# Moving the softmax weights and one combine of a two-part decode attention ahead of the last V group

## Chip, cores, metric

One core of a Trainium2 chip. The metric is device time in microseconds (us) of one execution. A time comes with a span, which is the time from the first to the last instruction of the core's profile. In all executions of this study the time is the span plus 1.7 to 2.0 us.

## The reference

Two decode attentions, A and B, each for one token. Each has 32 query heads, 16 key/value heads, head size 128 and model size 576. B attends to all 8192 cached positions, A to the last 2048. The outputs are concatenated.

```python
q = (x @ wq).reshape(B, Sq, Hq, Dh).transpose(0, 2, 1, 3)
k = repeat(k_cache[:, :, Sk - W:, :], rep)      # A: W = 2048; B: everything
v = repeat(v_cache[:, :, Sk - W:, :], rep)
p = softmax(einsum("bhqd,bhkd->bhqk", q, k) * Dh ** -0.5)
o = einsum("bhqk,bhkd->bhqd", p, v)
out = o.transpose(0, 2, 1, 3).reshape(B, Sq, Hq * Dh) @ wo
```

The inputs that must be read are 102.8 MB, nearly all of it K and V.

## The kernel before

The kernel streams K and V in slots of 2 MB, four slots to a group, five groups (A is group 0, B is groups 1 to 4). All loads are issued from one queue (SP). PE, the matmul engine, runs the groups in a loop. The loop has an inner part for K (transposes and scores, under a condition) and an outer part for V:

```python
inner = sorted(p for p in body if body[p].loop[2] is not None)
with eng.Fori(0, self.outer) as v:
    with eng.Fori(*self.rounds_of(v)) as g:
        while inner:
            ...                                  # K parts, each under its condition
    some(sorted(p for p in body if body[p].loop[2] is None))   # the V group
```

After each V group, DVE (the vector engine) extracts the useful blocks from PSUM (the memory that PE writes to) into `acc`:

```python
def v_keep(g):
    def go(dve): ...                             # diag <- opsum * mask, 0.69 us
    add("dve", go, reads=[B_O, "rows"], writes=[("diag", g % 2)])
    sums(acc[:, g, :], diag[:, g % 2, :, :], ...)  # acc <- diag, 0.69 us
```

Softmax statistics of each chunk are known long before. `weights(P)` turns them into factors. It is a chain of tiny steps that go back and forth between PE, DVE and ACT (the scalar engine):

```python
def weights(P):                                  # cut to the steps
    add("pe", ... misc[0:1, 0:128] <- transpose of the chunk maxima)
    add("dve", ... maximum over partitions); add("dve", ... scale, 4 small ops)
    add("pe", ... misc[:, 128:129] <- back to partitions); add("dve", ... copy)
    add("act", ... exp); add("dve", ... times the sums)
    add("pe", ... misc[:, 130:131] <- total over partitions)
    add("dve", ... reciprocal); add("dve", ... factors)
```

`combine(P)` scales and adds `acc` of the chunks on DVE, and gathers the heads with four fp32 matmuls. `wo_part` is the output projection, 128 short matmuls for each of A and B. Everything after the loop stands in this order:

```python
for P, lo, n, view, res, after in wo_loads:      # 3 loads of A's wo, 6 of B's
    load_wo(P, lo, n, view, res, after)          # into K and V slots that are free
weights(0)
weights(1)
for P in range(2):
    combine(P)
    for Q, lo, n, view, res, after in wo_loads:
        if Q == P:
            wo_part(P, lo, n, view, res)
    finish_out(P)
```

## Time and profile before

| | before |
|---|---|
| time, median of the first 3 runs (lowest to highest) | 251.45 us (251.21 to 251.67) |
| time of the run that was profiled | 252.97 us |
| span of the profiled run | 251.2 us |
| loads | 102.77 MB |
| last load lands | 245.30 us |

First the profile's slices, of the kernel before: busy tenths of PE, then the granted PE clock (tenths of full speed), the DMA engines' busy share (tenths) and the rate, in 40 slices of 6.3 us.

```profile
PE   0183799984999359995999349996353433543766
PEclk9999689999999759999999857999659555555556
DMA  7999999999999999999999999999999999999980
GB/s 274 396 432 422 432 425 428 417 436 428 428 427 423 428 420 436 421 431 428 431 423 431 431 431 423 431 431 428 425 428 436 423 433 425 433 418 425 423 332 3
```

The loads run at one rate from the second slice to the last but two.

Next the chain that ended last, of the kernel before: start us, us, what.

```profile
225.92 0.69 DVE acc L366
...
232.58 1.02 PE misc L597 x4
...
234.31 1.93 PE misc L620 x8
...
236.60 4.05 PE ktps L636 x120
...
242.40 1.93 PE misc L620 x8
...
244.68 4.06 PE ktps L636 x96
...
248.76 0.31 DVE outsb L642
```

The last V group has been extracted at 226.6. The weights of A and B take until 234.0, A's combine (L620) until 236.5, A's projection (L636) until 240.65; then the same two for B. The output store follows the last line. All of this is compute. No load stands in this chain.

Last, the loads of B's wo, of the kernel before: the first line has the shortest, median and longest time of issue (ns), then the first and last issue (us); the second the time from issue to landing.

```profile
L373 SPq DMA_DIRECT2D vslots<-in_B_wo_dram x5: 327/433/4230, 210.8 to 216.4; - x5
...
DMA to landing us min/median/max: 28.8/30.1/32.0
```

The last of these five, issued at 216.4, lands 28.9 us later, at 245.3: it queues behind other loads, of which the one before it lands at 244.95. The projection of B, which needs it, begins its first matmul at 244.68 and needs the last piece at about 248.6.

### The profile page before, as it was taken

The page shows a single profiled execution, that of the slowest core. Times are in us where ns is not written, and L with a number is a line of the kernel's source. Part 1 is how long each engine was busy: PE and PEld are TensorE (multiplying, and loading weights), DVE is VectorE, ACT ScalarE, POOL GpSimd, SP SyncE. Part 2 cuts the span into 40 slices and gives each one's busy share as a digit, 9 for nine tenths or more (in the row PEclk, how much of TensorE's full clock was granted, in tenths as well). Part 3 has the DMA queues.
Part 4 walks back from the last instruction along what each step waited for, and adds up shares of the span by engine and source line. Part 5 has one row for each costly group of instructions (what it writes and reads, how often), then busy time and mean ns, then how long its engine had stood idle before and what let it go on. Part 6 is the DMA issues. An engine that isn't in the chain of part 4 may idle for free. (4 is left out here: it accounts for less than half of the span.)

```text
span 251.2 us, 7501 instructions
## 1 busy us (share of the span) xinstructions
PE 167.9 (67%) x3406; PEld 130.6 (52%) x3406; DVE 80.6 (32%) x152; ACT 86.7 (35%) x92; POOL 12.9 (5%) x49
## 2 busy tenths in 40 slices
PE   0183799984999359995999349996353433543766
PEld 0031287764776358865776349783242322432755
DVE  0000244664653035554654024653031020014120
ACT  2000067839683027877676007874000000000000
POOL 7501000000000000000000000000000000000000
PEclk9999689999999759999999857999659555555556
DMA  7999999999999999999999999999999999999980
GB/s 274 396 432 422 432 425 428 417 436 428 428 427 423 428 420 436 421 431 428 431 423 431 431 431 423 431 431 428 425 428 436 423 433 425 433 418 425 423 332 3
DMA packets 8235, 102.92 MB, mean 410 GB/s; under 512 B 1184, under 2 KB 1312, under 8 KB 2080
## 3 DMA queue, kind: packets, MB, share of 16 engines
q1 hardware_dynamic: 7936, 102.77, 96.7%
q8 instruction: 8, 0.13, 0.2%
q10 hardware_dynamic: 288, 0.00, 0.1%
q14 instruction: 3, 0.02, 0.0%
HBM read 102.76 MB, written 0.00 MB: 409 GB/s over the span
## 5 line engine op out<-in xcount | busy, mean ns | idle before, releaser
L465 ACT ACTIVATE kt<-ktps 128x1024 bf16<-128x1024 bf16 x80 | 77.5, 1021 | 53.2 <-PE ktps L459 53.2
L459 PEld LDWEIGHTS ktps<-ident,kslots 128*128 128x128 bf16 x1280 | 76.3, 101 | 28.8 <-issue 28.8
L459 PE MATMUL ktps<-ident,kslots 128*128 128x128 bf16 x1280 | 82.4, 226 | 12.8 <-PEq L213 12.8
L468 DVE COPY kt<-ktps 128x1024 bf16<-128x1024 bf16 x80 | 55.2, 691 | 52.1 <-PE ktps L459 52.0
L550 PE MATMUL opsum<-vslots,ptm 128*32 128x128 bf16 x1280 | 29.9, 268 | 39.7 <-PEq L213 39.3
L550 PEld LDWEIGHTS opsum<-vslots,ptm 128*32 128x32 bf16 x1280 | 26.3, 121 | 44.2 <-issue 44.1
L479 PE MATMUL sacc<-kt,qst 128*32 128x512 bf16 x320 | 25.9, 392 | 2.0 <-PEq L213 1.8
L559 DVE TENSOR_TENSOR diag<-opsum,rows 128x512 f32<-128x512 f32 x5 | 3.5, 691 | 68.0 <-PE opsum L550 68.0
L589 ACT ACTIVATE stat<-stat 128x1 f32<-128x1 f32 (+1 forms) x2 | 0.6, 295 | 56.7 <-DVE stat L587 56.7
L418 PE MATMUL opsum<-vslots,xpad 128*32 128x512 bf16 x64 | 8.3, 497 | 16.1 <-DVE xpad L403 12.2
L418 PEld LDWEIGHTS opsum<-vslots,xpad 128*32 128x32 bf16 x64 | 2.2, 116 | 18.9 <-issue 13.1
L450 POOL COPY qst<-qtm 128x64 bf16<-128x64 bf16 x20 | 4.5, 236 | 122.8 <-PE sacc L479 113.3
L479 PEld LDWEIGHTS sacc<-kt,qst 128*32 128x32 bf16 x320 | 5.4, 94 | 8.7 <-issue 4.8
L424 ACT ACTIVATE qrow<-opsum 128x512 bf16<-128x512 f32 x2 | 1.2, 597 | 24.8 <-PE misc L418 24.8
L516 ACT ACTIVATE psb<-sacc,stat 128x2048 bf16<-128x2048 f32 x3 | 5.9, 1967 | 8.5 <-DVE stat L510 8.5
L418 PE MATMUL misc<-vslots,xpad 128*32 128x512 bf16 x64 | 8.4, 500 | 0.0
L426 DVE CAST qrow<-misc 128x512 bf16<-128x512 f32 x2 | 1.4, 690 | 16.2 <-PE misc L418 16.2
L636 PE MATMUL ktps<-kslots,opj 128*32 128x144 bf16 x184 | 5.9, 326 | 0.7 <-DVE opj L624 0.7
L636 PEld LDWEIGHTS ktps<-kslots,opj 128*32 128x32 bf16 x184 | 5.4, 146 | 1.0 <-issue 1.0
L620 PE MATMUL misc<-acc,pick 128*128 128x32 f32 x16 | 3.8, 404 | 2.5 <-DVE acc L614 1.8
L620 PEld LDWEIGHTS misc<-acc,pick 128*128 128x128 f32 x16 | 3.6, 328 | 2.9 <-DVE acc L614 2.1
L508 DVE TENSOR_REDUCE stat<-sacc 128x1 f32<-128x1024 f32 x3 | 3.7, 1225 | 1.8 <-PE sacc L479 1.8
(66 smaller groups left out, 57.7 us busy)
## 6 DMA issues: line engine op xcount, KB each, us to landing
kslots<-in_B_k_cache_dram SPq DMA_DIRECT2D x16, 2048.0 KB, 21.4
vslots<-in_B_v_cache_dram SPq DMA_DIRECT2D x16, 2048.0 KB, 18.1
kslots<-in_A_k_cache_dram SPq DMA_DIRECT2D x4, 2048.0 KB, 30.0
vslots<-in_A_v_cache_dram SPq DMA_DIRECT2D x4, 2048.0 KB, 24.7
vslots<-in_A_wq_dram SPq DMA_DIRECT2D x2, 2048.0 KB, 10.0
vslots<-in_B_wq_dram SPq DMA_DIRECT2D x2, 2048.0 KB, 20.2
kslots<-in_A_wo_dram SPq DMA_DIRECT2D x2, 2016.0 KB, 23.8
kslots<-in_B_wo_dram SPq DMA_DIRECT2D x1, 2016.0 KB, 31.2
```

The costliest lines, as they stand in the source:

```text
L418: ins = pe.matmul(qps[c][32 * j:32 * j + 32, :], lhsT=xpad[:, P, x, :], rhs=src[:, o:o + 512], start=(u == 0), stop=(u == WQ_UNITS - 1))
L450: add("pool", lambda pool: pool.tensor_copy(qst[:, s * 64:(s + 1) * 64], qtm[:, o:o + 64]), reads=[("qtm", KIND[g])], writes=[("qst", s)], ...
L459: ins = pe.matmul(ktps_bf[q][:, t * 128:(t + 1) * 128], lhsT=kslots[:, s, o:o + 128], rhs=ident[:, :], start=True, stop=True, is_transpose ...
L465: add("act", lambda act, q=q, dst=dst: act.activation(dst, ktps_bf[q], ACT.Copy), reads=[("bank", q)], writes=[("kt", u % NKT, q)], tag="e ...
L468: add("dve", lambda dve, q=q, dst=dst: dve.tensor_copy(dst, ktps_bf[q]), reads=[("bank", q)], writes=[("kt", u % NKT, q)], tag="e%d%d" % ( ...
L479: ins = pe.matmul(sacc[32 * j:32 * j + 32, 512 * half:512 * half + 512], lhsT=qst[:, s * 64 + e * 32:s * 64 + e * 32 + 32], rhs=rhs, start ...
L508: add("dve", lambda dve: dve.tensor_reduce(st(P, C_M + k), sacc[:, :], AX.X, ALU.max), reads=B_S, writes=[("st", P, C_M + k)], tag="max")
L516: return act.activation(psb[:, :].rearrange("p (x g) -> p x g", g=2), src, ACT.Exp, bias=st(P, C_NB + k), scale=SCALE, accum_out=st(P, C_L ...
L550: ins = pe.matmul(opsum[32 * j:32 * j + 32, s * DH:(s + 1) * DH], lhsT=ptm[:, o:o + 32], rhs=vslots[:, s, b * 128:(b + 1) * 128], start=(u ...
L559: return dve.tensor_tensor(diag[:, g % 2, :, :], opsum[:, :].rearrange("p (s d) -> p d s", s=NS), m, ALU.mult)
L620: ins = pe.matmul(misc[:, 0:32], lhsT=pick[:, r, :], rhs=acc[:, d, 32 * r:32 * r + 32], start=(r == 0), stop=(r == 3))
L636: ins = pe.matmul(ktps[P][32 * j:32 * j + 32, 0:OUTW], lhsT=opj[:, P, jj:jj + 32], rhs=view[:, o:o + OUTW], start=(jj == 0), stop=(jj == H ...
```

## The change

The weights of A and B and A's combine need nothing from the last V group. The change places them ahead of it. PE is then waiting for V loads anyway (in the profile of the kernel before it stands idle for 2.7 to 3.3 us ahead of each of the last four V slots). Since PE runs a loop, they become a conditional part of the loop's outer body, taken only in the last round. B's combine now comes before A's projection. No load and no arithmetic is added or removed. The core of the diff:

```diff
-            inner = sorted(p for p in body if body[p].loop[2] is not None)
+            def parts(of, i):
+                ...                          # runs of places with the same condition
+                        with eng.If(cond(i)):
+                            some(todo[:n])
             with eng.Fori(0, self.outer) as v:
                 with eng.Fori(*self.rounds_of(v)) as g:
-                    while inner:
-                        ...
-                some(sorted(p for p in body if body[p].loop[2] is None))
+                    parts("inner", g)
+                parts("outer", v)
 ...
+    LAST = lambda v: v == 4
     def weights(P):
+        at = [(6, 18 + P + k / 8, LAST, "outer") for k in range(3)]
 ...                                          # loop=at[0], at[1], at[2] on its three PE steps
-        add("pe", mm, reads=["pick", ("acc", d)], writes=[B_M])
+        add("pe", mm, reads=["pick", ("acc", d)], writes=[B_M], loop=(6, 19.5, LAST, "outer") if P == 0 else None)
 ...
+        if g == 6:
+            weights(0)
+            weights(1)
+            combine(0)
         if g in V_OF:
             for s in range(NS):
                 v_slot(V_OF[g], s, 20 + s, g)
 ...
-    weights(0)
-    weights(1)
+    combine(1)
     for P in range(2):
-        combine(P)
         for Q, lo, n, view, res, after in wo_loads:
```

The rest of the diff lets the bookkeeping of the loop's semaphore waits cope with the new places.

More of the change, by code (lines that the diff above doesn't have):

```diff
@@ L134, in waits_of_loop @@
     def waits_of_loop(self, ops):
-        points, state, tried = {}, [], {}
+        points, state, body = {}, [], {op.loop[1] for op in ops}
         for op in ops:
@@ L145, in waits_of_loop, with fits @@
             dma = key[0] == "dma"
-            runs = {p: sum(1 for q, _, _ in state if q == p) for p in places}
-            taker = max(places, key=lambda p: (runs[p], p))
-            def fits(first, n):
+            runs = {p: sum(1 for q, _, _ in state if q == p) for p in body}
+            def fits(first, n, places, taker):
                 took = 0
@@ L175, in waits_of_loop @@
                 continue
-            fit = [(first, n) for n in (1, 2, 16) for first in (0, n) if fits(first, n)]
+            also = places | {op.loop[1] for op in ops if any(o.key == key for o in op.deps)}
+            fit = [(first, n, some, taker) for some in (places, also) for taker in sorted(some, key=lambda p: (-runs[p], -p))
+                   for n in (1, 2, 16) for first in (0, n) if fits(first, n, some, taker)]
             assert fit, (key, places, [(p, k.get(key, 0), w.get(key)) for p, k, w in state if p in places])
-            first, n = fit[0]
+            first, n, places, taker = fit[0]
             if first:
@@ L216, in some @@
                     one(eng, body[place])
-            inner = sorted(p for p in body if body[p].loop[2] is not None)
+            def parts(of, i):
+                todo = sorted(p for p in body if body[p].loop[3] == of)
+                while todo:
+                    cond = body[todo[0]].loop[2]
+                    n = next((k for k, p in enumerate(todo) if body[p].loop[2] is not cond), len(todo))
+                    if cond is None:
+                        some(todo[:n])
+                    else:
+                        with eng.If(cond(i)):
+                            some(todo[:n])
+                    todo = todo[n:]
             with eng.Fori(0, self.outer) as v:
                 with eng.Fori(*self.rounds_of(v)) as g:
-                    while inner:
-                        cond = body[inner[0]].loop[2]
-                        n = next((k for k, p in enumerate(inner) if body[p].loop[2] is not cond), len(inner))
-                        with eng.If(cond(g)):
-                            some(inner[:n])
-                        inner = inner[n:]
-                some(sorted(p for p in body if body[p].loop[2] is None))
+                    parts("inner", g)
+                parts("outer", v)
         def run(name, eng):
@@ L461, in tr @@
                 return ins
-            add("pe", tr, reads=[("k", s), "ident"], writes=[("bank", q)], loop=(g, place + q / 8, K_ON))
+            add("pe", tr, reads=[("k", s), "ident"], writes=[("bank", q)], loop=(g, place + q / 8, K_ON, "inner"))
             dst = kt[:, u % NKT, q * 1024:(q + 1) * 1024]
@@ L483, in k_scores @@
         add("pe", mm, reads=[("qst", s)] + [("kt", u % NKT, q) for q in range(4)], writes=[B_S[half]],
-            loop=(g, place, K_ON))
+            loop=(g, place, K_ON, "inner"))
     def scores_zero(loop):
@@ L492, in mm @@
                 return ins
-            add("pe", mm, reads=["zero"], writes=[B_S[h]], loop=loop and (loop[0], loop[1] + h / 8, loop[2]))
+            add("pe", mm, reads=["zero"], writes=[B_S[h]], loop=loop and (loop[0], loop[1] + h / 8) + loop[2:])
     C_M, C_NB, C_L, C_W, C_AL, C_T = 0, 2, 4, 6, 8, 10
@@ L531, in tr @@
                 return ins
-            add("pe", tr, reads=["psb", "ident"], writes=[bank], loop=(g, place + u / 8, ODD))
+            add("pe", tr, reads=["psb", "ident"], writes=[bank], loop=(g, place + u / 8, ODD, "inner"))
             def put(dve, u=u, dst=dst):
@@ L553, in mm @@
             return ins
-        add("pe", mm, reads=[("ptm", 0), ("ptm", 1), ("v", s)], writes=[B_O], loop=(g, place, None))
+        add("pe", mm, reads=[("ptm", 0), ("ptm", 1), ("v", s)], writes=[B_O], loop=(g, place, None, "outer"))
     def v_keep(g):
@@ L571, in weights @@
         add("pe", lambda pe: pe.matmul(misc[0:1, 0:128], lhsT=st(P, m), rhs=identf[:, :], start=True, stop=True),
-            reads=[("st", P, m), "identf"], writes=[B_M])
+            reads=[("st", P, m), "identf"], writes=[B_M], loop=at[0])
         add("dve", lambda dve: dve.tensor_reduce(srow[0:1, P, 0:32],
@@ L585, in weights @@
                                        start=True, stop=True),
-            reads=[("srow2", P), "ones"], writes=[B_M])
+            reads=[("srow2", P), "ones"], writes=[B_M], loop=at[1])
         add("dve", lambda dve: dve.tensor_copy(st(P, C_T + 1), misc[:, 128:129]),
@@ L599, in total @@
             return ins
-        add("pe", total, reads=[("st", P, C_T + 2), "same"], writes=[B_M])
+        add("pe", total, reads=[("st", P, C_T + 2), "same"], writes=[B_M], loop=at[2])
         add("dve", lambda dve: dve.reciprocal(st(P, C_T + 4), misc[:, 130:131]),
@@ L680, in bass_concat_heads__sliding_block_cached__gqa_block_cached__decode_kernel @@
             softmax_transpose(g, 2)
-            scores_zero((g, 2.5, ODD))
+            scores_zero((g, 2.5, ODD, "inner"))
         if g < 5:
```

## The prediction

> **What bounds the kernel.** Loads, nearly to the end. By stretches of 25 us, the DMA share is 1.00 to 1.01 at 425 to 429 GB/s from 25 to 225 us. [...] PE is busy 67% of the span and waits in the V groups. By issue and landing times, the four last V slots land at 208.43, 213.32, 218.22 and 223.11 us, A's wo at 227.93, 232.76 and 234.19, B's wo at 239.00, 241.79, 243.21, 244.23, 244.95 and **245.30**. All are issued by 220.66, into a backlog.
>
> The chain of waits nevertheless ends in compute: V matmuls to 225.17, extraction to 226.6, weights of A and B in series to 234.0, A's combine to 236.5, A's projection 236.60 to 240.65, B's combine to 244.55, B's projection 244.68 to 248.74, copy 0.31, output store issued 249.10, end 251.2. Compute ends about 3 us later than the last load needs.
>
> **What the change moves.** No load, matmul or vector operation is added or removed. The weights, A's combine and the vector and scalar work between them go ahead of the last V group; on PE they stand in a conditional part of the loop, and B's combine now precedes A's projection. That takes about 9.8 us (226.6 to 236.4) off the chain after the last V slot. PE's loop gains one conditional per round, a few tenths of a microsecond at most (my estimate; the existing ones show no larger gap), which the loads hide.
>
> **The new time line** (durations of the trace, shifted): extraction of group 3 ends 207.03, weights and A's combine run to 216.7. The V slots that landed at 208.4 and 213.3 wait for that; then the group catches up at 1.9 us a slot: 218.7, 220.6, 222.5, and the last, landed 223.11, ends about 225.2 as before. B's wo loads into those V slots are issued 5 to 8 us later (from 218.7 and 220.7 instead of 210.8 and 215.4), but their data starts to move only at 239, so the queue does not run dry. Extraction to 226.6, B's combine to 230.2, A's projection follows its loads to 234.7, B's starts at 239.1 and follows its loads.
>
> The last load then sets the end: 245.30 + 0.14 (landing to matmul, as at V's last slot) + 0.43 (last head's four matmuls) + 0.02 + 0.31 (copy) + 0.04 + 2.07 (store, issue to end, as before[...]) = 248.3 us span, against 251.2: 2.9 us less. Of 9.8 us taken off the chain, 2.9 are gained; the rest becomes waiting for wo.
>
> **Predicted:** 251.45 - 2.9 = 248.6 us; 8 in 10 between 247.8 and 249.6. Faster by over 2% (under 246.4) would need the last load to land 2 us earlier, which nothing here causes: 0.03. Within 2%: 0.96. Slower: 0.01.
>
> **What would show it.** Right: the last load lands at 245 to 245.6; the weights stand at 205 to 217 us; PE waits for wo loads ahead of the projections; the chain ends in a load, four matmuls, a copy and the store; DMA share stays 1.0 to 243; the last V matmuls end within 0.5 us of 225.2.
>
> **What would make it wrong.** The later release of V slots 0 and 1 leaving a hole in the load queue (last landing after 246); [...]the first output store, queued behind loads, holding up the end; the last pieces' waits costing more than 0.14 us each.

Where the recorded texts, here and below, said something of the hardware that no trace or run of this case shows, it is cut and the cut marked. No term of the forecast's sum is among the cuts: all of them stand, and it came to 248.3 us of span.

## More of the kernel before

PE is far from full in the last third, and in the last nine slices its clock is at 5 to 6 tenths of full speed.

## The result

| | before | changed |
|---|---|---|
| time, median of 4 runs (lowest to highest) | 251.33 us (250.98 to 251.67) | 249.94 us (249.46 to 250.19) |
| ratio | | 0.9942 (95%: 0.9921 to 0.9964) |
| span of the profiled run | 251.2 us | 247.7 us |

A ratio here is the mean time of one kernel's fast runs over that of the other's in the same rounds, so it is not quite the ratio of the medians. The change gains, but the time is 0.3 us above the predicted range, and the gain is half of the predicted one. At the same time the two profiled spans differ by 3.5 us, which is more than predicted. These three facts have to be brought together.

The slices of the changed kernel:

```profile
PE   0193589994999559995999638998345144685634
PEclk9999959999799979998899955999858755557555
DMA  7999999999999999999999999999999999999993
GB/s 270 406 433 431 430 431 421 426 423 429 431 425 429 426 421 431 422 431 434 423 429 429 423 431 429 426 437 426 429 429 423 431 426 429 434 427 427 421 406 138
```

The loads run at the same rate, and now to the last slice. The chain of the changed kernel:

```profile
206.46 0.60 PE misc L581 x2
...
214.88 1.92 PE misc L630 x8
...
220.75 23.73 DMA vslots<-in_B_wo_dram
...
244.52 0.71 PE ktps L646 x12
...
245.26 0.31 DVE outsb L652
```

Weights and A's combine stand at 206.46 to 216.80, beside V loads. The chain now ends in a load, 12 matmuls and the copy. Its 23.73 us of "DMA" should be read with care. It counts from the issue of the piece, and the piece is issued late because its V slot is freed late. The loads of B's wo show that this lateness costs nothing:

```profile
L380 SPq DMA_DIRECT2D vslots<-in_B_wo_dram x5: 328/432/433, 218.7 to 221.2; - x5
...
DMA to landing us min/median/max: 22.7/23.7/31.2
```

They are issued 5 to 8 us later than before and land that much sooner after issue. The last lands at 244.85 here and at 245.30 before. PE's waits in the changed kernel, from 200 to 252 us (engine and line, waited for: us in total, times, longest):

```profile
PE ktps L646 <- DMA kslots<-in_B_wo_dram: 3.9, 1, 3.9
...
PE ktps L646 <- DMA kslots<-in_A_wo_dram: 1.9, 1, 1.9
...
PE ktps L646 <- DMA vslots<-in_B_wo_dram: 1.7, 4, 0.9
```

PE waits for wo for 7.5 us in its projections. The kernel is now bound by its loads to the end.

### The profile page after: what moved, and what is told of

It is laid out like the page before. It is cut to its first block, busy times and chain, and to the rows that moved or that the text cites. A ratio compares the mean times of both kernels' runs of the same rounds, so it can differ in the third digit from the quotient of the medians.

```text
span 247.7 us, 7505 instructions
## 1 busy us (share of the span) xinstructions
PE 169.6 (68%) x3406; PEld 132.3 (53%) x3406; DVE 81.0 (33%) x152; ACT 87.1 (35%) x92; POOL 12.9 (5%) x49
## 5 line engine op out<-in xcount | busy, mean ns | idle before, releaser
L466 PEld LDWEIGHTS ktps<-ident,kslots 128*128 128x128 bf16 x1280 | 78.9, 103 | 27.9 <-issue 27.9
L466 PE MATMUL ktps<-ident,kslots 128*128 128x128 bf16 x1280 | 85.1, 230 | 12.4 <-PEq L214 12.4
L557 PE MATMUL opsum<-vslots,ptm 128*32 128x128 bf16 x1280 | 28.1, 262 | 28.0 <-PEq L214 23.7
L557 PEld LDWEIGHTS opsum<-vslots,ptm 128*32 128x32 bf16 x1280 | 25.3, 119 | 31.6 <-issue 31.6
L486 PE MATMUL sacc<-kt,qst 128*32 128x512 bf16 x320 | 25.3, 392 | 1.8 <-PEq L214 1.8
L652 DVE CAST outsb<-ktps 128x144 bf16<-128x144 f32 x2 | 0.6, 307 | 16.0 <-PE ktps L646 16.0
```

The costliest lines, as they stand in the source:

```text
L466: ins = pe.matmul(ktps_bf[q][:, t * 128:(t + 1) * 128], lhsT=kslots[:, s, o:o + 128], rhs=ident[:, :], start=True, stop=True, is_transpose ...
L486: ins = pe.matmul(sacc[32 * j:32 * j + 32, 512 * half:512 * half + 512], lhsT=qst[:, s * 64 + e * 32:s * 64 + e * 32 + 32], rhs=rhs, start ...
L557: ins = pe.matmul(opsum[32 * j:32 * j + 32, s * DH:(s + 1) * DH], lhsT=ptm[:, o:o + 32], rhs=vslots[:, s, b * 128:(b + 1) * 128], start=(u ...
```

## The experiments

Theory G (clock). The tail of the kernel before is PE work, and its length depends on the clock granted there (in that kernel's profile the 64 matmuls of a V slot take 1.90 us at a clock of 0.50, and 1.08 at 1.00), and this clock changes from run to run. The profile used for the prediction was of a run in which the tail fell at half clock throughout. The gain over an ordinary run is smaller. Rivals: S, the load stream of that run was late; O, the profiled run has a different overhead around the span. A separate question is which part of the change earns the gain.

### Both kernels again (`ctl_before`, `ctl_after`, `ctl_after_2`)

No edit. The first two ran together on one chip, the third later on another.

> The kernel before, unchanged, to see its ordinary executions: the one profile on hand was taken of a run of 252.97 us (span 251.2), 1.5 us over the median of its other runs, and the prediction took a span difference from it. Theory G (clock): time minus span is a constant 1.8 us, ordinary spans lie at 249.2 to 250.0, and they vary by up to 2 us from run to run because the tail after the last V slot is PE work[...]: in a profile with a shorter span, part of the two projections shows a clock of 1.0 and each takes 2.3 to 3.5 us instead of 4.05, while the last load still lands at 244.8 to 245.5. Rival S (stream): a shorter span comes with an earlier last landing (by the same 1 to 2 us), at clock 0.5 in the whole tail. Rival O (overhead): spans stay at 251 and time minus span is about 0.3 us in ordinary runs.

> The changed kernel, unchanged. All theories: about 249.9 us, load-bound to the end. G: spans within 0.6 us of each other (247.7 to 248.3), a narrower spread than the kernel before has, since only four matmuls follow the last load; ratio to before 0.994. S: as wide a spread as before. O: time minus span differs from before's by over 1 us.

> The changed kernel again, beside the run above on the same chip, and for the ratio to before on another set of before's runs: 249.8 us, spans 247.7 to 248.4; ratio 0.991 to 0.994 depending on which of before's 249.0 to 251.5 us spans turn up.

Measured: before 252.04 us median of 6 (251.71 to 252.93; another 11 runs in the same rounds 251.94, 250.94 to 253.0). Changed 249.82 us of 6 (249.53 to 250.22), ratio 0.9915 (0.9887 to 0.9943); in the third run 249.74 us of 5 (249.58 to 249.89), ratio 0.9934 (0.9919 to 0.9949). Time minus span is 1.7 to 1.9 us for both, so rival O falls.

Over three sets of rounds I have 40 executions of the kernel before and, with the first result, 15 of the changed one. Spans: before 249.0 to 251.5 us, median 249.95; changed 247.7 to 248.4, median 248.0. The spread of the kernel before is 2.5 us, that of the changed kernel 0.7 us. The span of 251.2 that the prediction started from is exceeded by one of the 40. The expectation of 249.2 to 250.0 for ordinary spans was too narrow.

The new profile of the kernel before has a span of 250.1, 1.1 us shorter, although its last load lands at 245.38, no earlier than the 245.30 of the first. So rival S falls. Where the 1.1 us lies is seen in the new profile's chain:

```profile
236.67 4.00 PE ktps L636 x128
...
242.41 1.09 PE misc L620 x8
...
243.87 3.83 PE ktps L636 x97
```

B's combine (L620) took 1.09 us instead of 1.93, and B's projection 3.83 instead of 4.06; A's projection stayed at 4.00. That is less than expected (2.3 to 3.5 us for each projection). The stretches of both profiles with the projections' instructions (stretch: length, busy time of PE with its matmuls, of weight loads, granted clock, DMA share, GB/s) say why. First the profile of the kernel before that the prediction used, then the new one:

```profile
236.00:241.00 5.00, 4.03 (x128) 3.77 (x128) 0.50 0.97 401
243.00:249.00 6.00, 4.03 (x128) 3.77 (x128) 0.51 0.16 57
```

```profile
236.00:241.00 5.00, 3.98 (x128) 3.77 (x128) 0.55 0.98 407
243.00:249.00 6.00, 3.80 (x128) 3.64 (x128) 0.72 0.16 58
```

In the trace's clock records the first run has 0.50 from 194.3 to 248.9 us, and the second has 1.00 for 240.46 to 243.87 and again from 247.28. All steps in these records are at multiples of 3.41 us from each other, and the only values are 0.50 and 1.00. What decides about a step is not in the records. That the steps fall differently against the kernel's tail is seen in these two traces. The other executions have no profile, so that the clock makes their whole spread is an inference, which the next experiment tests.

### The cause by intervention (`warm_tail`)

In the first profile of the kernel before, the clock is 1.00 from 100 to 125 us, where PE is busy for 21.97 of the 25 us, and 0.50 from 200 to 225, where it is busy for 10.01 (but it is also 1.00 from 0 to 25, with 8.93). That more work on PE raises the clock is my guess, which this run tests. If it does, and the half clock makes the tail of the kernel before long, then keeping PE busy in the tail's gaps should shorten it, though it adds work. This kernel is the one before, with 13 matmuls of zeros into a PSUM bank that nobody reads:

```diff
+    def keep_warm(n):
+        def mm(pe):
+            for _ in range(n):
+                ins = pe.matmul(ktps[2][:, :], lhsT=ident[:, :], rhs=zero[:, :], start=True, stop=True)
+            return ins
+        add("pe", mm, reads=["ident", "zero"], writes=[("bank", 2)])
 ...
+        keep_warm(4 if P == 0 else 1)      # after the first PE step of weights(P)
+        keep_warm(1)                       # after its second and its third
 ...
+        if P == 0:
+            keep_warm(4)                   # after A's projection
```

> The kernel before with 13 idle matmuls (128x512, zeros times identity, into a PSUM bank that nobody reads) in PE's gaps of the tail: four while the last V group is extracted, one after each further weights step, four while B's combine is scaled. They add work and no result. Theory G (the tail's length in the kernel before is set by the half clock that the throttle grants PE there): the clock is 1.0 for most of the tail, each projection takes 3.2 us or so instead of 4.05, the combines 1.1 instead of 1.9, and the time falls from 252.0 to 249.9 to 250.8, span 248.1 to 249.0, with a narrower spread. Rival (the clock does not matter, or is not to be had by this): the added matmuls only cost, and the time is 252.0 to 253.5.

Measured: 249.76 us median of 6 (249.70 to 250.50), ratio to before 0.9911 (0.9875 to 0.9948), spans 247.9 to 248.6. The kernel before, with useless work added and nothing moved, is as fast as the changed kernel, and its spans lie within 0.7 us, where those of before in the same rounds lie between 249.0 and 251.5. The chain of its profile, and the projections' instructions in the window of the second projection (columns as above):

```profile
233.68 1.93 PE misc L630 x8
...
235.97 4.05 PE ktps L646 x119
...
241.77 1.09 PE misc L630 x8
...
243.23 2.12 PE ktps L646 x124
...
245.36 0.28 PE ktps L646 x4
245.66 0.31 DVE outsb L652
```

```profile
243.00:249.00 6.00, 2.37 (x128) 2.06 (x128) 0.93 0.14 53
```

Against the first profile of before, A's combine starts 0.63 us earlier, B's combine takes 1.09 instead of 1.93, and B's projection 2.40 instead of 4.06: 0.63 + 0.84 + 1.66 = 3.1 us, the whole difference of 251.2 and 248.1. In its clock records the clock is 1.00 from 241.38 to 248.21 us; in the first profile of before it is 0.50 until 248.93. The expectation was off in details: A's combine and projection stayed at half clock, at full clock a projection takes 2.4 us and not 3.2, and the time lies 0.1 us below the expected 249.9 to 250.8. The last load of this run lands at 245.32 and PE is done at 245.64, so the kernel is at its loads here too. Theory G holds: the clock in the tail is what the time of the kernel before depends on. The added matmuls also shift all later PE instructions, and such a shift moved a stop of PE by 32 matmuls in `reorder_shift64` below, but the stop that it moves there is in neither profile of the kernel before.

### Which part of the change earns it (`weights_only`, `reorder_only`)

`weights_only` is the changed kernel with A's combine moved back, and with it the old order of the tail:

```diff
-        add("pe", mm, ..., loop=(6, 19.5, LAST, "outer") if P == 0 else None)
+        add("pe", mm, ...)
-            combine(0)                      # ahead of the last V group
 ...
-    combine(1)
     for P in range(2):
+        combine(P)
```

> The changed kernel with A's combine moved back behind the loop and in before's order (combine A, project A, combine B, project B); only the weights stand in the loop's conditional part. Worked out from the trace of before: A's combine ends 229, A's projection follows its loads to 234.7, B's combine ends 238.7, and B's first wo piece lands at 239.0: still load-bound. Expected equal to the changed kernel within 0.2 us (249.9); if moving A's combine is worth something, 0.5 us or more slower.

Measured: 249.94 us median of 6 (249.75 to 250.15), ratio 0.9917 (0.9890 to 0.9944), beside 249.82 for the changed kernel in the same rounds. Moving A's combine and putting B's combine first are worth nothing on top of moving the weights.

`reorder_only` is the kernel before with only the order of the tail changed:

```diff
+    combine(0)
+    combine(1)
     for P in range(2):
-        combine(P)
         for Q, lo, n, view, res, after in wo_loads:
```

> The kernel before with one thing changed: B's combine is placed ahead of A's projection; weights stay after the loop and the loop is unchanged. If the gain is only the compute chain falling below the last load, this gains nearly as much: with the tail cold throughout, weights end 234.0, combines about 238.4, projections 242.4 and 246.5, span about 248.9; under theory G the second projection runs partly at full clock[...] and the span is 248.0 to 248.5, so the time is 249.8 to 250.4, within 0.3 us of the changed kernel. Rival: the weights' move is what matters, then this gains under 0.4 us (over 250.9).

Measured: 251.36 us median of 7 (251.05 to 253.05), ratio 0.9973 (0.9945 to 1.0001); that is not clear of no change. The expectation missed by 1 us, and the time lies in the range of its rival. There is one profile, of the slowest of these runs (span 251.2; the other six have 249.2 to 249.8). There B's combine ended at 239.6 us and not at 238.4 (DVE began to scale B only at 236.23, after its copy of A's result at 236.12), and the dense projections fell short. PE's lines in time:

```profile
239.57 4.01 PE L636 MATMUL ktps<-kslots,opj 128*32 128x144 bf16 x162
245.65 0.91 PE L636 MATMUL ktps<-kslots,opj 128*32 128x144 bf16 x22 [2.08 <-issue]
246.24 2.48 PE L636 MATMUL ktps<-vslots,opj 128*32 128x144 bf16 x72
```

PE stops for 2.08 us after 162 of 256 matmuls, in the midst of a tile that landed at 238.85 (B's first wo piece), waiting for nothing that the profile shows. In the packets, a read of 16,384 bytes on the instruction queue runs from 243.14 to 244.20. How long the other six runs stopped is not known.

### Is that stop an instruction fetch? (`reorder_shift64`)

The same kernel with 32 tiny matmuls at the very start of PE's program, where PE has nothing to do. A matmul is a weight load and a multiply (the profile of the kernel before has 3406 of each), so all later PE instructions stand 64 further on.

```diff
+    def shift(pe):
+        for _ in range(32):
+            ins = pe.matmul(ktps[2][0:32, 0:32], lhsT=zero[:, 0:32], rhs=zero[:, 0:32], start=True, stop=True)
+        return ins
+    add("pe", shift, reads=["zero"], writes=[("bank", 2)])
```

> The reordered kernel's profile has PE idle 2.08 us in the midst of the projections, after the 162nd of 256 matmuls, waiting for nothing the profile shows, while a 16 KB instruction read (243.14 to 244.20) runs under the loads. This kernel is the reordered one with 32 tiny matmuls at PE's start, where it idles: all later PE instructions stand 64 further on, if a matmul counts as a weight load and a multiply. Theory F (instruction fetch): the stall moves to about the 130th matmul, and the instruction read with it, about 1 us earlier; the time is about the same (251.0 to 251.5). Rival (a semaphore or a load): the stall stays after the 162nd matmul, where B's first wo piece is half used.

Measured: 250.38 us median of 4 (250.17 to 250.60), ratio 0.9928 (0.9881 to 0.9975), spans 248.2 to 248.6. PE's lines:

```profile
239.68 3.45 PE L636 MATMUL ktps<-kslots,opj 128*32 128x144 bf16 x130
243.99 1.05 PE L636 MATMUL ktps<-kslots,opj 128*32 128x144 bf16 x54 [0.85 <-issue]
244.82 1.35 PE L636 MATMUL ktps<-vslots,opj 128*32 128x144 bf16 x72
```

The stop moved from the 162nd to the 130th matmul, exactly 32 earlier, and the instruction read came with it (now at 241.51). So the stop is tied to a place in PE's instruction stream and not to a load or a semaphore. The time was expected to stay (251.0 to 251.5) and came out lower. The two profiles differ by 2.6 us of span: the stop is 1.2 us shorter, and the last 72 matmuls took 1.35 instead of 2.48 us, at a clock of 1.00. Whether the shift itself makes the kernel faster is not shown: the two ratios to before (0.9973 and 0.9928) have overlapping intervals. But it shows that the order alone, when the stop is short, comes within 0.6 us of the changed kernel. In the kernel before, PE pauses between the projections (idle for 1.77 and 0.37 us, around B's combine) and no such stop is in its traces. The stop was 2.08 us in one profile and 0.85 in the other, and 1.46 in that of `delay_10us` below. In the three, PE goes on 2.51, 2.48 and 2.36 us after the read begins, and the stop begins 0.43, 1.62 and 0.90 us after it: the stop is short where the read began early. PE also goes on 1.3 to 1.5 us after the read's last byte; what it waits for then, and what starts the read, stays open. That the stop is the wait for this read is therefore likely and not shown.

### How much room the changed kernel has (`delay_4us`, `delay_10us`)

The changed kernel with 6, or 14, useless DVE copies of 0.69 us between the extraction of the last V group and B's combine:

```diff
+    for i in range(6):                      # 14 in delay_10us
+        add("dve", lambda dve, i=i: dve.tensor_copy(kt[:, i // 4, i % 4 * 1024:i % 4 * 1024 + 1024], ktps_bf[2]),
+            reads=[("bank", 2)], writes=[("kt", i // 4, i % 4)])
     combine(1)
```

> The changed kernel with six useless copies on DVE (0.69 us each, 4.2 us together) between the extraction of the last V group and B's combine. If the changed kernel is load-bound, PE's waits for the wo pieces (1.9 + 3.9 + 1.7 us in its trace, 7.5 together) absorb it: 249.9 us, within 0.2. If compute still sets the end, 254.

> The same with 14 copies (10 us), about what the change took off the chain. 7.5 us of it should be absorbed: B's combine ends about 238.8, the projections 242.8 and 246.8 at half clock, so 1.2 us more than the changed kernel (251.1), up to 2 us more on top[...] as in the reordered kernel (253). If load-bound is wrong: 260.

Measured: 249.93 us of 4 (249.69 to 250.22) and 249.80 us of 4 (249.57 to 250.29), both equal to the changed kernel. The expectation for 10 us was 1.3 us too high. It reckoned both projections at half clock. With 10 us of delay they stand back to back and more than half of their matmuls run at the full clock (1.00 from 241.29 to 248.12 in that trace; 60 of them take 1.16 us there, where 72 take 2.40 at 0.50 in the first profile of the kernel before), and even a stop of 1.46 us, at the 162nd matmul as above, was absorbed. PE's lines, first of `delay_10us`, then of the changed kernel:

```profile
235.99 1.91 PE L630 MATMUL misc<-acc,pick 128*128 128x32 f32 x8 [11.24 <-DVE acc L624]
...
243.67 0.55 PE L646 MATMUL ktps<-kslots,opj 128*32 128x144 bf16 x22 [1.46 <-issue]
```

```profile
226.76 1.92 PE L630 MATMUL misc<-acc,pick 128*128 128x32 f32 x8 [2.87 <-DVE acc L624]
```

B's combine starts 9.2 us later than in the changed kernel's profile (235.99 against 226.76), and the time does not move. So the changed kernel has at least 9 us of room on the path from the last V group to the output.

### The load stream itself (`x_on_sp`)

At the floor of the loads, only the loads can be improved. The two tiny x loads go to the same queue as the large ones, behind the first of them:

```diff
-        add("act", go, writes=[("xtwo", P)], dma="x%d" % P)
-    load_x(0)
-    load_x(1)
+        add("sp", go, writes=[("xtwo", P)], dma="x%d" % P)
 ...                                        # load_x(0), load_x(1) after the first wq load
```

> The experiments so far say that the changed kernel is at the floor of its load stream, so only the stream itself can make it faster. Its trace has the loads running from 1.4 us, and a hole at 2 to 3 us (DMA share 0.24, 82 GB/s), just when the two tiny x loads are issued from ACT beside the first large loads. Here the x loads are issued on the same queue as the large ones, behind the first of these. If the x loads make the hole, it closes or shrinks, every landing comes up to 0.7 us earlier, and the time is 249.1 to 249.5 against 249.8; if not, 249.8, within 0.2.

Measured: 249.81 us of 6 (249.58 to 250.02), against 249.74 for the changed kernel in the same rounds. No gain. The hole at 2 to 3 us was there in both profiles (DMA share 0.37 here, 0.39 in the changed kernel of these rounds; 0.24 to 0.51 in four profiles without this edit). So the issue of the x loads from ACT is not what makes it. The x loads themselves are not ruled out: on the SP queue they are issued at 1.19 and 1.89 us, still ahead of the hole, and they put off the second large load from about 1.2 to 2.61 us. What makes the hole is open. No kernel here beats the changed one.

## Why the prediction was wrong

**The step that failed** is the last line of the sum, "251.45 - 2.9 = 248.6 us". Its 2.9 is the difference of two spans, 251.2 and 248.3, in which the 251.2 is of an execution that took 252.97 us. The 251.45 is the median of other executions, whose spans are about 1.8 us below their times, so about 249.6. A difference taken from a long execution was subtracted from an ordinary one. Taken from its own execution, 252.97 - 2.9 gives 250.1; measured were 249.94. Under it lies the premise that the durations of the one trace (4.05 us for a projection, 1.93 for a combine) were the kernel's own. They were those of half clock throughout. Over 40 runs the span before has a median of 249.95 us, so the ordinary gain is 249.95 - 248.0, about 2.0 us. The first 4 runs of before were on the short side, which gave 1.4 us; whether by chance or by the chip they ran on is not shown.

**The end of the changed kernel was right.** Predicted span 248.3; measured 247.7 to 248.4, median 248.0. Two terms differ in its profile. The last load landed at 244.85 instead of 245.30, just outside the predicted 245 to 245.6 (245.13 and 245.17 in the two later profiles of this kernel), and PE began 0.04 us after the landing of the last but one piece, not 0.14. The store took 2.07 us as predicted (245.59 to 247.66).

**Load-bound to the end was right**, and so was the warning of a hole in the load queue as the thing to look for: later issue cost nothing. The two delay runs show it by experiment.

**The weights' place was right** (206.46 to 216.80 against 205 to 217). The end of the last V group came at 223.90 and not within 0.5 us of 225.2. After three V slots in a row the clock records show 1.00 from 222.14 to 225.56 us, and the last slot took 1.08 us instead of 1.90. Nothing depended on it.

**The conditional** was put at a few tenths of a microsecond, my estimate from the existing ones in the profile of the kernel before: there PE goes on from the last scores of each of the five K groups, to the next K part or to the V group, in 0.10 to 0.23 us (53.78 to 54.01, 79.25 to 79.36, 113.14 to 113.34, 137.35 to 137.45, 171.53 to 171.68). In the last round PE stands still for 1.32 us between the last V matmul of one group and the first weights matmul (205.15 to 206.46), and 1.27 to 1.32 us in five other traces with this loop. This covers the loop's turn and the skipped K parts as well as the new condition; their shares were not separated. It is hidden under the loads: the last one landed at 244.85 all the same.

**Where the expected gain went.** 9.8 us left the chain. At half clock in the whole tail, some 3 us of it were above the floor of the loads. In ordinary runs the clock had already given back about 1 us of these (1.1 us in the second profile of the kernel before; for runs without a profile this is inferred). The rest became waiting for wo. The gain is a move from a compute-bound end that varies by 2.5 us to a load-bound end that varies by 0.7 us. Thirteen idle matmuls buy the same.

## What to carry to other kernels

Before subtracting a difference read in a profile from a median, compare the profiled execution's own time with that median; if they differ, the difference belongs to the profiled execution only. Where a chain of PE work sets the end and its clock is at half, expect the time to vary from run to run (here spans from 249.0 to 251.5 us), and expect part of any gain there to be absorbed already; once the chain is below the last load, nothing more is to be had from it (here the changed kernel took 9 us of added delay without a change in time). A late issue was harmless here because the queue had a backlog (issued 5 to 8 us later, the last load landed at 244.85 instead of 245.30): look at landings, not at issues.
